# A two-layer gated network behind retention attention: own buffers in the opening, sums on another engine, other steps for weight preparation

## The chip, the cores and the metric

The kernel runs on one core of a Trainium2 chip. The metric is the time of one execution on the device, in microseconds. The engines are TensorE (PE, with its weight loads shown apart as PEld), VectorE (DVE), ScalarE (ACT), GpSimd (POOL) and SyncE (SP), which issues most transfers.

## The reference, cut to what matters

Everything is float32, weights come as float64. First comes attention with a decay, no softmax (4 batches, 8 heads, 576 positions, 64 features), whose output, laid side by side, is x with 2304 rows of 512:

```
scores = (q @ k.T) / sqrt(64)
x = (scores * Dmat) @ v           # Dmat[i, j] = gamma[h] ** (i - j) for i >= j, else 0
```

The first layer has 1536 hidden features, the second 2048:

```
xn  = x / sqrt(mean(x * x) + 1e-6) * rms_g
g   = xn @ w_gate
x   = (g * sigmoid(g) * (xn @ w_val)) @ w_out
h   = x @ w_in
g   = where(h >= 1, h, where(h <= -1, 0, (h + 1) ** 2 / 4))
out = g @ w_out2
```

## The kernel before

Attention runs in chunks of 128 positions (a tail of 64 ends each batch), 20 chunks in all, with a running `state` for each head. A chunk has two loads of 512 KB: load 2i holds q and k by feature, load 2i+1 holds k and v by position. `scores` of a chunk multiplies k with q on PE, scales q and k by powers of the decay on POOL (`qs`, `ks`) and multiplies the scores by the decay matrix on DVE (`ret`). `values` does the products with v and the state, copies x to `xraw` and adds up its squares (`sums`).

The first layer runs over five blocks of 512, 512, 384, 512 and 384 tokens, and for each block over 12 slices of 128 hidden features, one `step_a` each. Every float32 product is three products of a high and a low part (`split`: a cast on ACT, a subtraction on DVE; `three`: the matmuls). A step does two products with the normed x (`front`), the gate, and the last step's products into four accumulators (`back_a`). In the first block the weights are converted from float64 (`convert`) and stored; later blocks load them again. `prepare_norm` works out the next block's norm in step 9 (`NORM`). The attention chunks that the next block needs are done in the steps of the block before it; those of the first block, and three more (`AHEAD`), in the opening, ahead of all steps.

The second layer's first product uses Strassen's algorithm in Winograd's form: seven products of half-size blocks, with sums of weights (`prepare_in`, four sums of 128x256) and sums of x (`sums_x`, four sums of 128x768 for each group of 768 tokens). `prepare_in` and `prepare_out` convert and split the second layer's weights while the first layer runs, and store them to `wfd` and `wod`. There are 16 calls, by turns one and the other. They share `wpair` (converted weights), `wsum` (sums) and `wprep` (split weights).

The program text is not the order of issue. `Plan` takes every operation down with its dependencies and an assumed cost, works out when each is due, counted back from its users, and then writes out each engine's order. It simulates the engines and takes, on the engine that is free first, the ready operation that is due first; on PE the one that comes first in the text. A cost for one engine doesn't depend on what another does at the time.

Buffers in the opening: `place` gives each of the 40 attention loads its buffer. The first 14 take five buffers in turn: the three of `att_p`, then `wpair` and `wsum`. The odd chunks of the opening have their `ret`, `qs` and `ks` in the four tiles of the ring `t0`, `t1` (`opening`), and `rms_tiles` takes two scratch tiles from the same ring:

```python
early = [*buffers, wpair, wsum]
place = [early[i % len(early)] if i < 2 * ahead else buffers[i % ATT] for i in range(2 * len(chunks))]
opening = [t_p.tile([P, 512], F32, tag=g, name=g)[:, :] for g in ("t0", "t0", "t1", "t1")]
ret_b = [[...], opening[:2]]
```

Of the kernel before, what the change touches and what calls it, by code (L numbers as in the profile page):

```python
# [2 lines left out]

# [7 lines left out]
F32 = mybir.dt.float32  # L11
# [8 lines left out]
NT, DM, FA, FB = B * S, H * D, 1536, 2048  # L20
P = 128
KD = DM // P
# [16 lines left out]
NORM = NA - 3  # L39
ATT = 3  # L40
STAGE = 3


class Ring:
# [166 lines left out]
def moe_chain_kernel(ctx: ExitStack, tc: tile.TileContext, att, tail, wa, wb, dmat, gq, gk, out):  # L211
    nc = Plan(tc.nc)
    pool = lambda name, bufs, **k: Ring(ctx.enter_context(tc.tile_pool(name=name, bufs=1, **k)), bufs)
# [4 lines left out]
    ret_p = pool("ret", 1)  # L218
    stage_p = pool("stage", STAGE)
    w_p = pool("w", 2)  # L220
    wt_p = pool("wt", 2)
    one_p = pool("one", 1)
    h_p = pool("h", 3)
    xraw_p = pool("xraw", 2)
    t_p = pool("t", 2)
    r_p = pool("r", 1)
    sum_p = pool("sum", 2)
    sq_p = pool("sq", 1)
    o_p = pool("o", 2)
    ps_p = pool("ps", 1, space=PSUM)  # L230
    fr_p = pool("fr", 2, space=PSUM)
    dram_p = pool("dram", 1, space=DRAM)
# [4 lines left out]
    eps = const.tile([P, 1], F32, name="eps")  # L237
    ones = const.tile([P, P], F32, name="ones")
    state = const.tile([P, NPAIR, P], F32, name="state")
    xall = one_p.tile([P, 14 * 2 * TB], F32R, name="xall")  # L240
    wprep = one_p.tile([P, 8 * DM], F32R, name="wprep")
    wpair_w = one_p.tile([P, 2 * DM], U32, name="wpair")
    wsum_w = one_p.tile([P, 2 * DM], U32, name="wsum")
    wpair, wsum = (a[:, :].bitcast(F32) for a in (wpair_w, wsum_w))
    wa32 = dram_p.tile([NA, P, 3 * DM], F32, name="wa32")
    wfd = dram_p.tile([NPB, P, 14 * 2 * P], F32, name="wfd")
# [5 lines left out]
    def need(t):  # L252
        end = STARTS[t] + BLOCKS[t]
        return sum(b * S + c * CH < end for b in range(B) for c in range(NCH))
# [4 lines left out]
    stage_t, loaded, taken = {}, [0], [0]  # L259
    stages = [stage_p.tile([P, DM, 2], U32, tag="stage", name="st") for _ in range(STAGE)]  # L260
    more = [*stages, *(a.rearrange("p (n w) -> p n w", w=2) for a in (wpair_w, wsum_w))]
    stage_of = [more[i % len(more)] if 9 <= i < 3 * NA - 2 else stages[i % STAGE] for i in range(len(slots))]

# [27 lines left out]
    def split(src, hi, lo):  # L291
        nc.scalar.copy(out=hi, in_=src)
        nc.vector.tensor_sub(out=lo, in0=src, in1=hi.bitcast(F32))
# [24 lines left out]
    def a_weights(s, j):  # L318
        hi, lo = wt_t[s][:, :3 * DM], wt_t[s][:, 3 * DM:6 * DM]
        return hi[:, j * DM:(j + 1) * DM], lo[:, j * DM:(j + 1) * DM]  # L320

    def prepare_in(p):

        convert(wpair, 2)
        n = 2 * P
        a11, a12, a21, a22 = (wpair[:, i * n:(i + 1) * n] for i in range(4))
        s2, s1, s3, s4 = (wsum[:, i * n:(i + 1) * n] for i in range(4))
        nc.gpsimd.tensor_add(out=s1, in0=a21, in1=a22)
        nc.gpsimd.tensor_sub(out=s2, in0=s1, in1=a11)
        nc.gpsimd.tensor_sub(out=s3, in0=a11, in1=a21)  # L330
        nc.gpsimd.tensor_sub(out=s4, in0=a12, in1=s2)
        ready = wprep[:, :14 * n]
        hl = ready.rearrange("p (j w n) -> p j w n", w=2, n=n)
        for src, j0, j1 in ((wpair[:, :2 * n], 0, 2), (wsum, 2, 6), (a22, 6, 7)):
            src = src.rearrange("p (j n) -> p j n", n=n) if j1 - j0 > 1 else src.unsqueeze(1)
            split(src, hl[:, j0:j1, 0], hl[:, j0:j1, 1])
        nc.sync.dma_start(out=wfd[p], in_=ready.bitcast(F32))
# [18 lines left out]
    chunks = [(b, c) for b in range(B) for c in range(NCH)]  # L356
    first, ahead = need(0), need(0) + AHEAD
    buffers = [att_p.tile([P, 8 * CH], F32, tag="att") for _ in range(ATT)]
    early = [*buffers, wpair, wsum]
    place = [early[i % len(early)] if i < 2 * ahead else buffers[i % ATT] for i in range(2 * len(chunks))]  # L360
    opening = [t_p.tile([P, 512], F32, tag=g, name=g)[:, :] for g in ("t0", "t0", "t1", "t1")]
    ret_b = [[ret_p.tile([P, 4 * CH], F32, tag=f"ret{h}", name="ret")[:, :] for h in range(2)], opening[:2]]
    qs_b = [qk_p.tile([P, 4 * CH], F32, tag="qs", name="qs")[:, :], opening[2]]
# [28 lines left out]
    xraw, sums = {}, {}  # L392

    def x_slice(t):
        if t not in xraw:
            xraw[t] = xraw_p.tile([P, KD, 512], F32, tag="xraw", name="xraw")
            sums[t] = sum_p.tile([P, 512], F32, tag="sum", name="sums")
        return xraw[t], sums[t]

# [90 lines left out]


    def rms_tiles(T):
        tiles = t_p.tile([P, 512], F32, tag="t0"), t_p.tile([P, 512], F32, tag="t1"), r_p.tile([P, 512], F32, tag="y")
        return [a[:, :T] for a in tiles]

    def rms_rstd(t, ps):

# [50 lines left out]
    def back_a(s, i):  # L548
        _, t, f = steps[s]
        T = BLOCKS[t]  # L550
        oh, ol = a_weights(s, 2)
        hh, hl = h_t[s]
        if f == 0 and i == 0:
            acc_t[t] = [ps_p.tile([P, 512], F32, tag=f"acc{i}") for i in range(KD)]
        ps = acc_t[t][i]
        q = slice(i * P, (i + 1) * P)
        three(ps[:, :T], oh[:, q], ol[:, q], hh[:, :T], hl[:, :T], f == 0, f == NA - 1)
        if f == NA - 1:
            o = o_p.tile([P, 512], F32, tag="o", name="o")
            nc.scalar.copy(out=o[:, :T], in_=ps[:, :T])  # L560
            nc.scalar.dma_start(out=x2d[:, i, STARTS[t]:STARTS[t] + T], in_=o[:, :T])

# [13 lines left out]
    def step_a(s):  # L576
        _, t, f = steps[s]
        T = BLOCKS[t]
        goal = goals[t] if f < NORM else 0
        weights_split(s + 1, 0)  # L580
        if t and f % 2 == 0 and f < 8:
            prepare()
        g = front(s, 0)
        att_step(goal, "values")
        u = t_p.tile([P, 512], F32, tag="t0", name="u")
        w = t_p.tile([P, 512], F32, tag="t1", name="w")
        nc.scalar.activation(out=u[:, :T], in_=g[:, :T], func=ACTF.Sigmoid)
        nc.vector.tensor_mul(out=u[:, :T], in0=g[:, :T], in1=u[:, :T])
        v = front(s, 1)
        att_step(goal, "scores")  # L590
        nc.vector.tensor_mul(out=w[:, :T], in0=v[:, :T], in1=u[:, :T])
        if f == NA - 1 and t + 1 < len(BLOCKS):
            split_x(t + 1, 0, KD)
        h = h_p.tile([P, 4 * TB], F32R, tag="h", name="h")
        h_t[s] = h[:, :512], h[:, 512:1024]
        split(w[:, :T], h[:, :T], h[:, 512:512 + T])
        if s:
            back_a(s - 1, 0)
            back_a(s - 1, 1)
            prepare_norm(s)  # L600
            back_a(s - 1, 2)
            back_a(s - 1, 3)
        weights_split(s + 1, 1)
        weights_f32(s + 2)
# [15 lines left out]
    def load_x2(b):  # L620
        x2_t[b] = []
        for j in range(2):
            x = xraw_p.tile([P, KD, 512], F32, tag="xraw", name="x2")
            at = (2 * b + j) * TB
            nc.sync.dma_start(out=x[:, :, :TB], in_=x2d[:, :, at:at + TB])
            x2_t[b].append(x)
# [3 lines left out]
    def sums_x(b):  # L630
        x1, x2 = x2_t[b]
        b11, b21, b12, b22 = (x[:, k:k + 2, :TB] for x in (x1, x2) for k in (0, 2))
        three_d = lambda a: a.rearrange("p (k n) -> p k n", k=2)
        t1, t2 = three_d(wpair[:, :2 * TB]), three_d(wsum[:, :2 * TB])
        nc.gpsimd.tensor_sub(out=t1, in0=b12, in1=b11)
        nc.gpsimd.tensor_sub(out=t2, in0=b22, in1=t1)
        nc.gpsimd.tensor_sub(out=b12, in0=b22, in1=b12)
        t4 = three_d(gq_sb[:, :2 * TB])
        nc.gpsimd.tensor_sub(out=t4, in0=b21, in1=t2)
        xb_t[b] = [b11, b21, t2, t1, b12, b22, t4]  # L640

    xs = xall.rearrange("p (j w k n) -> p j w k n", w=2, k=2, n=TB)
# [24 lines left out]
    def back_b(q, i):  # L667
        b, p = divmod(q, NPB)
        if p == 0 and i == 0:
            acc_t["B", b] = [ps_p.tile([P, 512], F32, tag=g) for g in ("acc0", "acc1", "acc2", "acc3", "at0", "at1")]  # L670
        ps = acc_t["B", b][i]
        j, r = i * P // TB, slice(i * P % TB, i * P % TB + P)
        for f in range(2):
            hh, hl = h_t["B", q, f, j]
            w = wo_t[q, f]
            three(ps, hh[:, r], hl[:, r], w[:, :DM], w[:, DM:], p == 0 and f == 0, p == NPB - 1 and f == 1)
        if (i + 1) * P % TB == 0:
            for f in range(2):
                h_room.append(h_t.pop(("B", q, f, j)))
        if p == NPB - 1:  # L680
            o = o_p.tile([P, 512], F32, tag="o", name="o")
            nc.scalar.copy(out=o, in_=ps)
            r0 = (b * MT + i) * P
            nc.scalar.dma_start(out=out[r0:r0 + P, :], in_=o)
# [10 lines left out]
    def step_b(q):  # L695
# [47 lines left out]
        if p == 0 and b + 1 < NSB:  # L743
            load_x2(b + 1)
            sums_x(b + 1)
# [11 lines left out]
    while load_att():  # L757
        pass
    for i in range(STAGE):
        load_slot()  # L760
# [110 lines left out]
```

## Time and profile before

| what | before |
|---|---|
| median of 3 runs | 954.89 us (954.47 to 955.55) |
| the profiled execution's own time | 955.68 us |
| its span | 953.5 us |
| mean granted clock of TensorE | 0.981 |
| PE busy | 919.0 us (96%) |
| DVE busy | 575.8 us (60%) |
| ACT busy | 481.5 us (50%) |
| POOL busy | 123.9 us (13%) |

All times of the trace come from one profiled execution; times within it are counted from the first instruction. The span is from the first to the last instruction. Busy shares are means over stages with different limits, so what an engine's idle time is worth is read from the waits of each stage. In the rows below nearly every instruction has line L134, the helper that issues all operations; they are told apart by their tiles, written as out<-in.

### The profile page before, as it was taken

To read this page: it belongs to the slowest core of one execution; us is meant where nothing else is said; L and a number is where in the kernel's file an instruction comes from. 1 tells how busy PE (TensorE), PEld (TensorE's weight loads), DVE (VectorE), ACT (ScalarE), POOL (GpSimd) and SP (SyncE) were. 2 spreads that over 40 slices of the span, in tenths; PEclk is the share of its full clock that TensorE was granted. 3 is DMA by queue.
4 is the path that set the end of the run, shared out by engine and by line. 5 is a ranking of instruction groups with operands and counts; after the bars stand their busy time and mean duration, and the time that the engine had idled before them with its cause. 6 is when DMAs were issued, how large, how long until landed. Compare 5 with 4: busy or idle time off the path is not lost.

```text
span 953.5 us, 13338 instructions
## 1 busy us (share of the span) xinstructions
PE 919.0 (96%) x5098; PEld 809.4 (85%) x5098; DVE 575.8 (60%) x875; ACT 481.5 (50%) x852; POOL 123.9 (13%) x124
## 2 busy tenths in 40 slices
PE   7689999999999899999998999999999999999997
PEld 7567888888889798888898998899989898989896
DVE  4787889787887789644658554433653345534342
ACT  3444566645666565533544445344655455644443
POOL 4531001430214410200003001200030000000000
PEclk9779999999999899999999999999999999999999
DMA  9787874998868975522235359455675554756431
GB/s 352 273 296 249 273 271 161 380 350 291 307 223 351 359 279 200 182 78 100 100 132 177 133 194 346 166 180 185 224 272 193 172 206 159 243 188 210 154 133 66
DMA packets 50782, 209.94 MB, mean 220 GB/s; under 512 B 5536, under 2 KB 9760, under 8 KB 46624
## 3 DMA queue, kind: packets, MB, share of 16 engines
q1 hardware_dynamic: 44528, 198.72, 58.5%
q10 hardware_dynamic: 6192, 10.38, 2.9%
q8 instruction: 40, 0.66, 0.3%
q14 instruction: 22, 0.18, 0.1%
HBM read 167.14 MB, written 41.94 MB: 219 GB/s over the span
## 4 chain that ended last, share of the span: by engine, by line
PE 87%; DVE 5%; DMA 4%; ACT 2%; issue 2%; POOL 1%; ACTq 0%; DVEq 0%; SPq 0%; POOLq 0%
PE fr L134 48%; PE acc L134 28%; PE at L134 12%; DMA att<-in_att_dram 2%; DVE wt L134 1%; DMA x2d<-o 1%; DVE xall L134 1%; ACT att L134 1%; DVE t L134 0%; DVE w L134 0%; DMA out_dram<-o 0%; DMA gk_sb<-in_gk_dram 0%; DVE h L134 0%; ACT o L134 0%; DVE wpair L134 0%
## 5 line engine op out<-in xcount | busy, mean ns | idle before, releaser
L134 PE MATMUL fr<-xall,wt 128*128 128x384 f32 (+1 forms) x2424 | 516.2, 359 | 10.6 <-DVE t L134 3.5
L134 PEld LDWEIGHTS fr<-xall,wt 128*128 128x128 f32 x2424 | 442.2, 190 | 60.9 <-DVE wt L134 4.2
L134 PE MATMUL acc<-h,wt 128*128 128x512 f32 (+1 forms) x708 | 159.6, 372 | 0.1
L134 PE MATMUL acc<-wprep,h 128*128 128x512 f32 x576 | 156.1, 394 | 2.2 <-DVE h L134 1.8
L134 PEld LDWEIGHTS acc<-h,wt 128*128 128x128 f32 x708 | 128.3, 188 | 19.1 <-issue 0.7
L134 DVE TENSOR_TENSOR wt<-w,wt 128x512 fp32r<-128x512 f32 (+1 forms) x118 | 120.4, 1039 | 22.6 <-ACT wt L134 22.5
L134 ACT CAST wt<-w 128x512 fp32r<-128x512 f32 (+1 forms) x118 | 96.7, 834 | 59.5 <-PE acc L134 32.6
L134 PEld LDWEIGHTS acc<-wprep,h 128*128 128x128 f32 x576 | 106.6, 188 | 18.1 <-DVE h L134 2.1
L134 DVE TENSOR_TENSOR t<-fr,t 128x512 f32<-128x512 f32 (+1 forms) x120 | 76.2, 635 | 74.9 <-PE fr L134 40.0
L134 ACT ACTIVATE att<-att 128x384 f32<-128x384 f32 x156 | 79.1, 523 | 30.8 <-DVE att L134 20.9
L134 ACT CAST h<-t 128x512 fp32r<-128x512 f32 (+1 forms) x60 | 34.6, 576 | 77.5 <-DVE t L134 77.5
L134 DVE TENSOR_TENSOR h<-att,h 128x384 fp32r<-128x384 f32 x96 | 56.3, 591 | 25.3 <-ACT h L134 24.7
L134 PE MATMUL at<-wprep,h 128*128 128x512 f32 x288 | 70.3, 392 | 0.0
L134 DVE TENSOR_TENSOR att<-fr,att 128x384 f32<-128x384 f32 x48 | 26.6, 555 | 71.6 <-ACT att L134 70.3
L134 ACT ACTIVATE t<-fr 128x512 f32<-128x512 f32 (+1 forms) x60 | 33.3, 555 | 64.3 <-PE fr L134 64.0
L134 PEld LDWEIGHTS at<-wprep,h 128*128 128x128 f32 x288 | 53.7, 188 | 10.3
L134 ACT COPY att<-fr 128x384 f32<-128x384 f32 x48 | 23.0, 479 | 75.2 <-PE fr L134 71.9
L134 ACT CAST h<-att 128x384 fp32r<-128x384 f32 x96 | 48.7, 511 | 23.7 <-DVE att L134 22.5
L134 DVE SCALAR_TENSOR_TENSOR att<-att,att 128x384 f32<-128x384 f32 x48 | 28.0, 583 | 42.6 <-ACT att L134 42.6
L134 DVE TENSOR_TENSOR h<-t,h 128x512 fp32r<-128x512 f32 (+1 forms) x60 | 40.6, 677 | 14.6 <-ACT h L134 14.4
L134 POOL TENSOR_TENSOR wpair<-xraw,xraw 128x768 f32<-128x768 f32 x3 | 5.7, 1887 | 271.5 <-DMA xraw<-x2d 167.7
L134 POOL TENSOR_TENSOR wsum<-wpair 128x256 f32<-128x256 f32 x16 | 16.7, 1045 | 134.0 <-ACT y L134 62.9
(130 smaller groups left out, 734.6 us busy)
## 6 DMA issues: line engine op xcount, KB each, us to landing
w<-wa SPq DMA_DIRECT2D x48, 768.0 KB, 4.6
wprep<-wod SPq DMA_DIRECT2D x48, 512.0 KB, 4.3
wt<-wfd SPq DMA_DIRECT2D x24, 1024.0 KB, 5.2
wt<-wfd SPq DMA_DIRECT2D x24, 768.0 KB, 4.4
stage<-in_wb_dram SPq DMA_DIRECT2D x32, 512.0 KB, 5.9
att<-in_att_dram SPq DMA_DIRECT2D x29, 512.0 KB, 7.5
wfd<-wprep SPq DMA_DIRECT2D x8, 1792.0 KB, 6.8
stage<-in_wa_dram SPq DMA_DIRECT2D x26, 512.0 KB, 4.9
```

The source lines that it names most:

```text
L134: call = lambda: getattr(real, method)(*args, **kwargs)
```

## The change

Five edits:

- The first eight attention loads (chunks 0 to 3) get eight places of their own: the five of before, the two halves of the second `xraw` tile, and `o_sb`. Loads 8 to 13 go on in turn through the first five.
- `o_sb`, one tile of two halves, takes the place of the two `o` tiles: `next(o_next)` hands out the halves by turns for results on their way out. `rms_tiles` takes its two scratch tiles from the halves of `o_sb` as well, not from `t0` and `t1`. The two `xraw` tiles are fixed by index instead of by the ring.
- The four sums of `prepare_in` are done on DVE, not on POOL.
- The four sums of `sums_x` are done on DVE, not on POOL.
- `PREPARE` lists, block by block, the steps in whose text a `prepare` call stands. Before, each block but the first had steps 0, 2, 4 and 6; now the five blocks have 0, 4, 2, 4 and 6 calls.

```diff
+PREPARE = [(), (1, 3, 5, 7), (5, 7), (1, 3, 5, 7), (0, 1, 2, 3, 5, 6)]
...
-    o_p = pool("o", 2)
+    o_sb = one_p.tile([P, 2 * DM], F32, name="o")
+    o_next = itertools.cycle((o_sb[:, :DM], o_sb[:, DM:]))
...
-        nc.gpsimd.tensor_add(out=s1, in0=a21, in1=a22)
-        nc.gpsimd.tensor_sub(out=s2, in0=s1, in1=a11)
-        nc.gpsimd.tensor_sub(out=s3, in0=a11, in1=a21)
-        nc.gpsimd.tensor_sub(out=s4, in0=a12, in1=s2)
+        nc.vector.tensor_add(out=s1, in0=a21, in1=a22)
+        nc.vector.tensor_sub(out=s2, in0=s1, in1=a11)
+        nc.vector.tensor_sub(out=s3, in0=a11, in1=a21)
+        nc.vector.tensor_sub(out=s4, in0=a12, in1=s2)
...
-    early = [*buffers, wpair, wsum]
-    place = [early[i % len(early)] if i < 2 * ahead else buffers[i % ATT] for i in range(2 * len(chunks))]
+    xraws = [xraw_p.tile([P, KD, 512], F32, tag="xraw", name="xraw") for _ in range(2)]
+    flat = xraws[1].rearrange("p k n -> p (k n)")
+    early = [*buffers, wpair, wsum, flat[:, :1024], flat[:, 1024:], o_sb[:, :]]
+    place = [early[i] for i in range(8)] + [early[i % 5] for i in range(8, 2 * ahead)]
+    place += [buffers[i % ATT] for i in range(2 * ahead, 2 * len(chunks))]
...
-            xraw[t] = xraw_p.tile([P, KD, 512], F32, tag="xraw", name="xraw")
+            xraw[t] = xraws[t % 2]
...
-        tiles = t_p.tile([P, 512], F32, tag="t0"), t_p.tile([P, 512], F32, tag="t1"), r_p.tile([P, 512], F32, tag="y")
-        return [a[:, :T] for a in tiles]
+        return o_sb[:, :T], o_sb[:, DM:DM + T], r_p.tile([P, 512], F32, tag="y")[:, :T]
...
-            o = o_p.tile([P, 512], F32, tag="o", name="o")
+            o = next(o_next)
...
-        if t and f % 2 == 0 and f < 8:
+        if f in PREPARE[t]:
             prepare()
...
-            x = xraw_p.tile([P, KD, 512], F32, tag="xraw", name="x2")
+            x = xraws[j]
...
-        nc.gpsimd.tensor_sub(out=t1, in0=b12, in1=b11)
-        nc.gpsimd.tensor_sub(out=t2, in0=b22, in1=t1)
-        nc.gpsimd.tensor_sub(out=b12, in0=b22, in1=b12)
+        nc.vector.tensor_sub(out=t1, in0=b12, in1=b11)
+        nc.vector.tensor_sub(out=t2, in0=b22, in1=t1)
+        nc.vector.tensor_sub(out=b12, in0=b22, in1=b12)
...
-        nc.gpsimd.tensor_sub(out=t4, in0=b21, in1=t2)
+        nc.vector.tensor_sub(out=t4, in0=b21, in1=t2)
```

## Rows read from the trace of the kernel before

**Rows 1.** The page, busy time, share of the span and instructions of an engine:
```profile
PE 919.0 (96%) x5098; PEld 809.4 (85%) x5098; DVE 575.8 (60%) x875; ACT 481.5 (50%) x852; POOL 123.9 (13%) x124
```
**Rows 2.** Waits of PE, 0 to 70 us: total, times, longest
```profile
PE at L134 <- DVE t L134: 4.1, 3, 3.3
PE at L134 <- DMA att<-in_att_dram: 2.2, 2, 1.6
```
**Rows 3.** Timeline of the opening: start, duration, instruction [idle before <-releaser]
```profile
11.60 1.56 SPq L134 DMA_DIRECT2D att<-in_att_dram  x3
...
19.88 1.79 PE L134 MATMUL acc<-ret,att 128*64 128x128 f32 x16 [0.97 <-DMA att<-in_att_dram]
...
38.68 1.74 DVE L134 SCALAR_TENSOR_TENSOR t<-t,t 128x512 f32<-128x512 f32 x1
40.34 1.27 DVE L134 TENSOR_TENSOR t<-acc,d_sb 128x512 f32<-128x512 f32 x2
...
41.12 1.12 PE L134 MATMUL acc<-att,t 128*64 128x64 f32 x16 [5.12 <-issue]
```
**Rows 4.** Waits of PE, 281 to 388 us, the third block
```profile
PE fr L134 <- ACT wt L134: 3.3, 1, 3.3
PE fr L134 <- DVE t L134: 1.8, 1, 1.8
PE fr L134 <- DVE wt L134: 1.6, 2, 1.5
```
**Rows 5.** Waits of PE, 485 us to the end
```profile
PE acc L134 <- DVE h L134: 1.8, 1, 1.8
PE fr L134 <- DVE t L134: 1.7, 2, 1.5
PE fr L134 <- DVE wt L134: 1.2, 1, 1.2
```
**Rows 6.** Windows: length, busy PE, PEld, DVE, ACT, POOL; granted clock, DMA share, GB/s
```profile
10.00:40.00 30.00, 20.62 (x242) 17.63 (x242) 21.03 (x31) 13.24 (x23) 18.59 (x20) 0.83 0.97 372
40.00:70.00 30.00, 23.92 (x195) 20.23 (x196) 26.02 (x40) 14.63 (x25) 9.28 (x11) 0.79 0.70 242
140.00:281.00 141.00, 141.00 (x780) 116.15 (x780) 119.98 (x170) 84.64 (x130) 32.93 (x35) 1.00 0.77 283
281.00:388.00 107.00, 100.18 (x684) 93.03 (x680) 85.65 (x126) 62.12 (x102) 30.91 (x31) 0.97 0.80 301
```
**Rows 7.** The chain that ended last, in order of time: start, duration, what
```profile
69.07 5.22 PE fr L134 x18
...
325.34 10.72 PE fr L134 x46
340.63 8.26 PE fr L134 x46
...
485.11 4.18 PE fr L134 x24
...
521.61 5.66 PE fr L134 x22
```
**Rows 8.** The same windows, instructions on tile wsum alone (columns as Rows 6)
```profile
140.00:281.00 141.00, 0.00 (x0) 0.00 (x0) 6.09 (x5) 5.25 (x5) 19.58 (x20) 1.00 0.77 283
281.00:388.00 107.00, 0.00 (x0) 0.00 (x0) 4.49 (x3) 3.14 (x3) 12.46 (x12) 0.97 0.80 301
```
**Rows 9.** Timeline, one DVE subtraction of 128x256
```profile
323.20 0.41 DVE L134 TENSOR_TENSOR wprep<-wpair,wprep 128x256 fp32r<-128x256 f32 x1
```
**Rows 10.** Timeline of POOL and DVE at the first big sums
```profile
510.49 1.85 POOL L134 TENSOR_TENSOR wpair<-xraw,xraw 128x768 f32<-128x768 f32 x1 [103.75 <-DVE h L134]
510.64 2.51 DVE L134 TENSOR_TENSOR xall<-xraw,xall 128x768 fp32r<-128x768 f32 x1 [0.18 <-ACT xall L134]
...
521.95 0.95 DVE L134 TENSOR_TENSOR xall<-wsum,xall 128x768 fp32r<-128x768 f32 x1
```
**Rows 11.** Tile wfd, its stores: duration min/median/max ns, first and last start us
```profile
L134 SPq DMA_DIRECT2D wfd<-wprep x8: 319/320/327, 163.6 to 360.0; - x8
```

More of the change, by code (lines that the diff above doesn't have):

```diff
@@ L1 @@
-import heapq
+import itertools
 from contextlib import ExitStack
@@ L680, in back_b @@
         if p == NPB - 1:
-            o = o_p.tile([P, 512], F32, tag="o", name="o")
+            o = next(o_next)
             nc.scalar.copy(out=o, in_=ps)
```

## The prediction

> **What bounds the kernel now.** I read the page's first part first: TensorE (PE) is busy for 919.0 us, 96% of the span [rows 1]. So the matmuls are the bound almost everywhere, and an edit that adds no matmul and removes none can win only where PE stands idle or runs at its lower clock. Next come the waits of PE, stretch by stretch; the reader is to see that the idle time sits in three places. Before 70 us 4.1 us are for DVE and 2.2 for `att` transfers [rows 2], and one wait of 5.12 us has no releaser that the profile shows ("issue") [rows 3]. In the third block of the first layer (281 to 388 us) PE waits 3.3 + 1.8 + 1.6 = 6.7 us, for ACT and DVE [rows 4]. From 485 us to the end there are three more, 1.8 + 1.7 + 1.2 = 4.7 us [rows 5]. Last I read the busy times by stretch [rows 6]: DVE is the fullest engine beside PE, 120.0 of 141 us in the second block and 85.7 of 107 us in the third, and PE is never idle in the second. The granted clock is 0.83 and 0.79 of full speed (2.4 GHz) in the two opening stretches, a mean over its two levels, and 1.00 in the second block.
>
> The profiled execution took 955.68 us, 2.1 us around its span, and lies 0.8 us above the median of the runs shown (954.89). The sum is made against 955.7 and 0.8 us are taken off at the end. A run of this kernel tells a change from none at about 0.2%, or 1.9 us.
>
> **Part 1: the opening.** Attention loads 0 to 4 have five places; loads 5, 6 and 7 (the v half of chunk 2, both halves of chunk 3) must wait until loads 0, 1 and 2 are used up. They are issued only at 11.60 us, behind three weight loads [rows 3], and PE waits 0.97 us at 19.88 for the first of them [rows 3]. With own places they depend on nothing, and the planner, which issues by due time, puts them ahead of the three weight loads, whose first matmul comes after all chunks of the opening. Three loads of 512 KB at the 372 GB/s of this stretch [rows 6] are 4.2 us: so much earlier they land, and so much later the three weight loads. The later weights are covered: the first long run of matmuls on them starts at 69.07 us [rows 7]. Of the 2.2 us the longest, 1.6 us [rows 2], is at chunk 0 and stays; 0.6 us is for load 6. With the 0.97 that makes 1.6 us.
>
> The second edit in the opening is that `rms_tiles` takes its two scratch tiles from `o_sb`, not from the ring `t0`, `t1`. Until now those scratch tiles are also the `ret` buffers of the odd opening chunks. The rows show what that costs: the scratch op runs at 38.68 for 1.74 us, the multiply of chunk 5 (t<-acc,d_sb) follows only at 40.34, and PE, which needs both halves of it, starts again at 41.12 after 5.12 us idle [rows 3]. With its own scratch that multiply can run as soon as its scores are there. But DVE is near full then, 26.0 us busy of 30 from 40 to 70 [rows 6], so the wait is partly replaced by its queue. Bounds: 0 (DVE sets the pace of the whole opening, and everything won waits for DVE again) and all 5.1. I take 2.5, half. Beside the longest (3.3) the 4.1 us for DVE hold 0.8 [rows 2]; 0.6 of it, as I read it, is chunk 3's state product behind its late scores; it goes with the late load. The opening gives 1.6 + 2.5 + 0.6 = 4.7 us. Bounds for all of it: 0, and 9.0, the idle time of DVE from 10 to 40 us (30 - 21.03) [rows 6].
>
> **Part 2: the sums go from POOL to DVE.** There are 32 sums of 128x256, 20 in the second block and 12 in the third, 32.0 us on POOL together [rows 8], and 12 of 128x768 (four for each of three groups of tokens). DVE shows no such op by itself; the nearest rows are its subtractions of the same shapes with two SBUF inputs, 0.41 us for 128x256 [rows 9] and 0.95 us for 128x768 [rows 10]. So DVE gets 32 x 0.41 = 13.1 and 12 x 0.95 = 11.4 us, 24.5 us in all. What it gets back: while POOL runs a sum, a DVE op with two SBUF inputs is held. POOL starts at 510.49 and is done 1.85 us later, at 512.34; the DVE subtraction that starts at 510.64 takes 2.51 us and ends at 513.15, 0.81 us after POOL, while the same shape takes 0.95 us at 521.95 [rows 10]. One sum here costs DVE 1.6 us where it would cost 0.95 us on DVE itself. For DVE as a whole I take the move as neutral (bounds: nothing given back, +24.5 us, and the 1.6-for-0.95 of this row everywhere). What changes for PE is where the delays fall: the planner knows the cost of a sum on DVE, but not that a POOL op holds DVE, and now urgent DVE ops are late by up to 1.6 us at a time.
>
> By stretch. At 510 us the four sums of the second layer's first x: PE waits 1.7 + 1.2 = 2.9 us [rows 5], and the 22 matmuls after it take 5.66 us where 24 take 4.18 [rows 7], part of them at the lower level of the clock, to which it fell after the idle time: 5.66 - 22/24 x 4.18 = 1.8 us. Of 4.7 us I take 4.0, since four DVE ops of 0.95 us now stand in that queue (bounds 0 and 4.7). The same four sums for the second group of tokens stand beside the 1.8 us wait for `h` [rows 5]; I take 1.3 (bounds 0 and 1.8).
>
> In the third block the waits are 6.7 us, and 46 matmuls after them take 10.72 us where the next 46 take 8.26 [rows 7]: 2.4 us at the lower clock, 9.1 us in all. The sums of three prepares fall there. But the longest wait, 3.3 us, is for an ACT cast: ACT stood in front of an early rms matmul, and that is the order written by the planner and not POOL. A new plan may have such a spot again. Bounds: 9.1 gained, and 3 lost (one more such wait); I take half, 4.5.
>
> **Part 3: the chosen steps.** I cost it at nothing. Program order only sets dependencies; the order of issue is by due time. The preparations depend on each other (`wpair`, `wsum`, `wprep`, the stages), not on the step in which they are written. The trace says so: a quarter of them are written into the last block, which starts at 485.1 us [rows 7], yet the last store of `wfd` is issued at 360.0 [rows 11]. If the steps did matter, two preparations fewer would fall into the third block; its 9.1 us is the bound on that side and 0 the other. The x tiles of fixed index and the one `o` tile keep two buffers each; no queue is passed.
>
> **Sum.** 4.7 + 4.5 + 4.0 + 1.3 = 14.5 us. 955.7 - 14.5 - 0.8 = 940.4 us; its own range is 936 to 947.
>
> **Rivals.**
> (a) The opening gives nothing since DVE paces it, and the new plan puts a stall into the third block again: only 4.0 + 1.3 = 5.3 us stay, 949.6 us. For it speaks DVE's 26 of 30 us in [rows 6]; against it the 9 us that DVE is idle before.
> (b) DVE becomes the bound. In the second block PE has no idle time at all [rows 6], so there is nothing to win, only to lose: 20 of the 32 small sums are there and 12 in the third block. If each stands ahead of an op that PE needs, PE loses 13.1 us; the gains of part 1 (4.7) and the 5.3 us of the big sums remain: 955.7 + 13.1 - 10.0 - 0.8 = 958.0 us. It decides once DVE has no gap left to take the sums: it has 21 us in each of the two blocks [rows 6], against 20 x 0.41 = 8.2 and 12 x 0.41 = 4.9 us of sums. The Trainium skill (Perfetto Trace Analysis, Optimizing Scalar/DVE Operations) says that with DVE saturated, moving work to ScalarE or even GpSimd may make sense, which is this change backwards; it adds that the two share a read port, so that it might not help. The trace agrees with the second half (the held subtraction above), and by the first half alone the time would be 958.0.
> (c) All the waits of the third block go, and the opening gains what DVE allows: 9.0 + 9.1 + 4.7 + 1.8 = 24.6 us, 930.3 us.
> (d) The planner's new order gives back what it gains: no change, 953 to 957.
>
> **Chances.** Forecast (936 to 947) 0.47, (a) (947 to 953) 0.20, (c) (under 936) 0.13, (d) 0.07, (b) 0.13. Faster by over 0.2%: 0.80; within: 0.07; slower: 0.13. The range is 930 to 955: below it a part of (c), above it (b) and the upper end of (d), together under 0.2.
>
> **What would show it.** Right: in the opening, the v load of chunk 2 landing ahead of the weights and no wait of PE for it; the multiply of chunk 5 not behind the scratch op; steady matmuls at least 4 us earlier. No DVE subtraction of 128x768 above 1 us near the big sums, and PE without a wait there. `wfd` stores at nearly the same times. Wrong: PE waits for DVE in the second block; a new wait for ACT in the third; or an opening that starts its long run of matmuls at 69 us as before.

## The result and the profile after

The changed kernel takes 923.56 us (922.26 to 923.88), a ratio of 0.9657 to the kernel before, interval [0.9628, 0.9687]: about 32 us less, where 14.5 were forecast. The sign was right, the size was not, and the time lies under the range.

The busy times by stretch (columns as [rows 6]), in the same two opening stretches, then the third block and the last block of the changed kernel:

```profile
10.00:40.00 30.00, 23.76 (x320) 19.21 (x320) 21.60 (x35) 15.24 (x29) 20.93 (x24) 1.00 0.92 339
40.00:70.00 30.00, 28.58 (x225) 23.03 (x226) 26.48 (x42) 14.82 (x26) 10.52 (x12) 1.00 0.68 234
260.54:385.98 125.44, 125.21 (x880) 115.30 (x879) 105.81 (x165) 74.19 (x123) 23.43 (x25) 1.00 0.74 272
460.11:537.11 77.00, 77.00 (x442) 76.49 (x440) 49.66 (x70) 36.47 (x59) 0.00 (x0) 1.00 0.49 166
```

The clock is at full speed in both opening stretches, against 0.83 and 0.79 in [rows 6], and PE has almost no idle time in the third block and none in the last. The waits of PE over the whole span of the changed kernel:

```profile
PE at L135 <- DMA att<-in_att_dram: 1.4, 1, 1.4
PE fr L135 <- DVE xall L135: 1.3, 1, 1.3
PE at L135 <- DVE t L135: 1.3, 1, 1.3
PE fr L135 <- POOL sum L135: 1.2, 1, 1.2
...
PE acc L135 <- ACT h L135: 0.5, 1, 0.5
...
PE fr L135 <- DVE wt L135: 0.2, 1, 0.2
```

All above 0.6 us are in the opening; of [rows 4] only 0.2 us for `wt` is left and of [rows 5] nothing. The timeline of the opening, changed kernel:

```profile
8.95 0.80 SPq L135 DMA_DIRECT2D xraw<-in_att_dram  x2
...
10.18 0.33 SPq L135 DMA_DIRECT2D o<-in_att_dram  x1
...
11.79 1.28 SPq L135 DMA_DIRECT2D stage<-in_wa_dram  x3
...
18.91 1.09 PE L135 MATMUL acc<-ret,xraw 128*64 128x128 f32 x16
...
25.80 1.13 PE L135 MATMUL fr<-sum,ones 128*128 128x512 f32 x2 [1.17 <-POOL sum L135]
...
28.36 1.28 DVE L135 TENSOR_TENSOR t<-acc,d_sb 128x512 f32<-128x512 f32 x2
...
29.56 0.68 DVE L135 SCALAR_TENSOR_TENSOR o<-o 128x512 f32<-128x512 f32 x1
...
35.74 0.96 PE L135 MATMUL fr<-xall,wt 128*128 128x512 f32 x3 [0.27 <-ACT xall L135]
```

Loads 5, 6 and 7 stand in SP's queue ahead of the three weight loads, PE has their data without a wait (18.91, against 0.97 us in [rows 3]), and the multiply of chunk 5 now stands ahead of the scratch op. The norm matmul of the first block (fr<-sum,ones) starts at 25.80; in the kernel before at 33.79.

For all comparisons below I count matmuls: a step of the first layer has 24 on `xall` (two products, four slices, three each), so step s begins with number 24s+1 of them. From the profiled runs, in us (blocks begin with steps 0, 12, 24, 36 and 48; the second layer is from step 60 on):

| kernel | ratio to before, interval | step 0 at | step 12 at | step 24 at | steps 24-39 | steps 48-60 | second layer |
|---|---|---|---|---|---|---|---|
| before | 1 | 45.7 | 163.7 | 276.8 | 134.0 | 82.5 | 386.1 |
| changed | 0.9657 [0.9628, 0.9687] | 35.7 | 150.1 | 260.5 | 125.4 | 77.0 | 383.4 |
| open_only | 0.9781 [0.9751, 0.9810] | 37.2 | 151.6 | 262.1 | 131.9 | 82.6 | 387.6 |
| place_only | 0.9792 [0.9766, 0.9819] | 37.8 | 151.6 | 264.1 | 128.0 | 82.6 | 389.4 |
| rms_only | 0.9938 [0.9915, 0.9962] | 45.3 | 160.4 | 273.3 | 132.3 | 83.7 | 387.5 |
| sums_only | 0.9866 [0.9844, 0.9889] | 45.9 | 163.9 | 278.6 | 131.1 | 77.0 | 383.2 |
| place_old | 0.9826 [0.9811, 0.9840] | 45.8 | 164.9 | 277.7 | 127.7 | 77.0 | 383.8 |
| pin_pool | 0.9689 [0.9673, 0.9705] | 35.7 | 150.0 | 260.4 | 128.1 | 77.0 | 383.5 |
| sx_pool | 0.9727 [0.9710, 0.9745] | 37.9 | 153.3 | 263.8 | 125.7 | 82.6 | 385.8 |
| fill_before | 0.9989 [0.9972, 1.0005] | 42.6 | 161.0 | 274.2 | 134.0 | 83.5 | 387.9 |
| late_issue | 0.9783 [0.9768, 0.9798] | 49.4 | 158.9 | 271.4 | 128.3 | 77.0 | 383.8 |
| weights_last | 0.9805 [0.9788, 0.9822] | 41.5 | 150.6 | 263.8 | 126.6 | 83.9 | 387.4 |
| wl_sums | 0.9683 [0.9662, 0.9705] | 42.9 | 151.9 | 264.4 | 125.5 | 77.5 | 383.3 |

Steps 39 to 48 take 74.1 us in each. The 33.0 us of span (953.5 to 920.5) are 16.3 up to step 24, 8.6 in steps 24 to 39, 5.5 in the last block and 2.6 in the second layer (before rounding). Up to step 24 PE is busy for 259.75 us of 276.82 before and 251.58 of 260.54 after, with the same 1578 matmuls: 8.1 us less idle time, and 8.2 us less for the same work, which I put down to the clock (granted 0.96 of full speed in that stretch before, 1.00 after).

The columns of times come from one execution each, and in the opening one execution does not repeat another. Kernels with the same order of instructions up to 144 us or more came as far apart as this at step 12: 150.0, 150.1, 151.6 and 153.3 us with the new order (pin_pool, changed, open_only, sx_pool); 162.6 to 165.0 with the old one (before, and three kernels further below that leave the opening alone); 160.4 and 164.9 in rms_only and place_old. The granted clock goes with it: 0.87 from 40 to 70 us in rms_only, 0.73 in place_old. So a difference of 10 us up to step 24 is one of the kernels, and a difference under some 4 us need not be. Where the order is the same, the stretches from step 24 to step 60 repeat within 1 us and the second layer within some 2 us.

### The profile page after: what moved, and what is told of

Read it like the earlier page. It is cut to its first block, busy times and chain, and to the rows that moved or that the text cites. A ratio compares the mean times of both kernels' runs of the same rounds, so it can differ in the third digit from the quotient of the medians.

```text
span 920.5 us, 13305 instructions
## 1 busy us (share of the span) xinstructions
PE 905.6 (98%) x5098; PEld 798.5 (87%) x5098; DVE 574.0 (62%) x919; ACT 480.5 (52%) x852; POOL 70.4 (8%) x80
## 4 chain that ended last, share of the span: by engine, by line
PE 92%; DMA 3%; DVE 2%; ACT 1%; issue 1%; POOL 0%; ACTq 0%
PE fr L135 50%; PE acc L135 30%; PE at L135 11%; DMA x2d<-o 1%; DMA att<-in_att_dram 1%; DVE xall L135 0%; DMA out_dram<-o 0%; DMA gk_sb<-in_gk_dram 0%; DVE xraw L135 0%; ACT o L135 0%; DVE t L135 0%; ACT att L135 0%; DVE w L135 0%; DVE wt L135 0%; DVE o L135 0%
## 5 line engine op out<-in xcount | busy, mean ns | idle before, releaser
L135 PEld LDWEIGHTS fr<-xall,wt 128*128 128x128 f32 x2424 | 437.3, 188 | 51.9 <-DVE xall L135 2.4
L135 PEld LDWEIGHTS acc<-h,wt 128*128 128x128 f32 x708 | 128.3, 188 | 18.2
L135 DVE TENSOR_TENSOR wt<-w,wt 128x1024 fp32r<-128x1024 f32 (+1 forms) x118 | 115.1, 987 | 25.1 <-ACT wt L135 24.5
L135 ACT CAST wt<-w 128x1024 fp32r<-128x1024 f32 (+1 forms) x118 | 96.9, 835 | 52.5 <-PE acc L135 30.0
L135 DVE TENSOR_TENSOR h<-att,h 128x384 fp32r<-128x384 f32 x96 | 52.8, 554 | 23.8 <-ACT h L135 23.2
L135 DVE SCALAR_TENSOR_TENSOR att<-att,fr 128x384 f32<-128x384 f32 x24 | 13.3, 554 | 35.3 <-ACT att L135 35.3
L135 DVE TENSOR_TENSOR xall<-xraw,xall 128x512 fp32r<-128x512 f32 (+2 forms) x32 | 26.0, 828 | 2.6 <-ACT xall L135 2.4
```

The costliest lines, as they stand in the source:

```text
L135: call = lambda: getattr(real, method)(*args, **kwargs)
```

## The experiments

### Which part does it

Three kernels with the changed places and the new scratch, both or one at a time, with sums on POOL and the old steps:

```diff
 open_only   # early, place, o_sb as changed; sums on gpsimd; f % 2 == 0 and f < 8
 place_only  # the same, and
-        return o_sb[:, :T], o_sb[:, DM:DM + T], y
+        return t0[:, :T], t1[:, :T], y      # the ring's tiles
 rms_only    # open_only, and
-    place = [early[i] for i in range(8)] + [early[i % 5] for i in range(8, 2 * ahead)]
+    place = [early[i % 5] for i in range(2 * ahead)]
```

> Only the opening is changed: own places for loads 0 to 7, and the scratch tiles of the norm in o_sb; all sums stay on POOL, the steps of the preparations are the old ones. Theory 1 (the parts act each in their own stretch): step 12 comes about 16 us earlier, as in the changed kernel, the granted clock stays at full speed in the opening, the later stalls stay (third block, last block): 936 to 940 us. Theory 2 (the new order of the whole plan made the gain, no part by itself): a time that has nothing to do with 16 us, under 5 us gained or over 25.

> Only the eight own places; the norm's scratch tiles stay in the ring t0, t1 and the sums on POOL. If the late loads were what made the opening slow: 8 us or more gained, step 0 at about 38 us. If the shared scratch was: under 4 us, and a long wait of PE behind the multiply of chunk 5 stays.

> Only the norm's scratch tiles move to o_sb; loads 5 to 7 wait for used places as before, sums on POOL. If the shared scratch made the opening slow: 8 us or more gained. If the late loads did: under 4 us, and step 0 no earlier than 43 us.

Measured: 21 us for both parts, 20 for the places alone, 6 for the scratch alone. The places make the opening. rms_only is the miss for my reading of [rows 3]: with a scratch of its own the multiply of chunk 5 still stands behind the scratch op on DVE, and PE waits just as long, 5.07 us. Its timeline:

```profile
37.75 1.44 POOL L135 TENSOR_TENSOR qs<-att,gq_sb 128x512 f32<-128x512 f32 x1
37.99 1.75 DVE L135 SCALAR_TENSOR_TENSOR o<-o 128x512 f32<-128x512 f32 x1
39.66 1.28 DVE L135 TENSOR_TENSOR t<-acc,d_sb 128x512 f32<-128x512 f32 x2
...
40.40 1.93 PE L135 MATMUL acc<-t,att 128*64 128x128 f32 x12 [5.07 <-DVE t L135]
```

What held the multiply was its place in DVE's queue, not the shared tile. In place_only, where the tile is still shared, the wait is gone. The rows show something more that the working had passed over: the scratch op takes 1.75 us here with a POOL op on two SBUF tensors beside it, and ends 0.55 us after that op; in the changed kernel, with POOL idle, the same op takes 0.68 (29.56 above). A part of this wait is POOL holding DVE, as with the sums below.

The sums alone, on the kernel before:

```diff
-        nc.gpsimd.tensor_add(out=s1, in0=a21, in1=a22)   # and the seven others
+        nc.vector.tensor_add(out=s1, in0=a21, in1=a22)
```

> The kernel before with the sums of weights and of x on DVE, nothing else. Theory 1: the opening is as slow as before (step 12 within 1 us of 163.7), the later waits go: 16 to 17 us gained, 937 to 940 us. Theory 2: stalls come back at other places in the third block, 945 us or more. The forecast's own term for this part was 9.8 us.

Measured 13 us (0.9866; 945.8 us beside a kernel before of 959.0), by its gain between the two expectations: the opening is unchanged (step 12 at 163.9), the last block takes 77.0 us and the second layer 383.2, as in the changed kernel, but the third block keeps 5.7 of its 8.6 us.

Three that undo one part of the changed kernel:

```diff
 pin_pool    # prepare_in: nc.vector back to nc.gpsimd
 sx_pool     # sums_x: nc.vector back to nc.gpsimd
 place_old   # place = [early[i % 5] for i in range(2 * ahead)], five places
```

> The changed kernel with the four sums of the weights back on POOL; the sums of x stay on DVE. If those sums make the waits of the third block: 5 to 7 us slower than the changed kernel (a ratio of about 0.972 to the kernel before), all of it between steps 24 and 39; last block and second layer as in the changed kernel. If they do nothing: within 1 us of the changed kernel (0.966).

> The changed kernel with the four sums of x back on POOL; the sums of the weights stay on DVE. If a POOL sum holds DVE: the last block (steps 48 to 60) takes 82.6 instead of 77.0 us and the second layer 386 to 388 instead of 383.4, so 8 to 10 us slower than the changed kernel (a ratio of about 0.975). If only the new order made that gain: under 4 us.

> The changed kernel with five places in turn for the first 14 loads, as before; the norm's scratch tiles stay in o_sb. If the late loads made the opening slow: step 12 at 160 us as with the scratch tiles alone, so 10 us slower than the changed kernel (a ratio of about 0.976). If the sums on DVE shorten the opening as well: 5 us or less.

pin_pool is 2.7 us longer in the third block and the same elsewhere: half of what was expected; over whole runs its interval overlaps that of the changed kernel. sx_pool has the last block back at 82.6 and the second layer at 385.8 us (8.0 together, as expected). Its step 24 comes 3.3 us late as well, but up to 380 us every engine has the same instructions in the same order as in the changed kernel: that is the difference between two executions, not an effect of the edit. place_old has the old opening, 164.9. Over all the kernels of the table the last block takes 82.5 to 83.9 us where the sums of x are on POOL and 77.0 to 77.5 where they are on DVE, and the second layer 385.8 to 389.4 and 383.2 to 383.8, whatever else differs. In sx_pool's timeline at these sums, first DVE, then POOL:

```profile
489.27 0.96 DVE L135 TENSOR_TENSOR xall<-xraw,xall 128x768 fp32r<-128x768 f32 x1 [0.18 <-ACT xall L135]
490.19 2.30 DVE L135 TENSOR_TENSOR wt<-w,wt 128x512 fp32r<-128x512 f32 x1
492.40 2.61 DVE L135 TENSOR_TENSOR xall<-xraw,xall 128x768 fp32r<-128x768 f32 x1
```
```profile
489.76 2.17 POOL L135 TENSOR_TENSOR wpair<-xraw,xraw 128x768 f32<-128x768 f32 x1 [104.87 <-DMA xraw<-x2d]
492.01 2.19 POOL L135 TENSOR_TENSOR wsum<-xraw,wpair 128x768 f32<-128x768 f32 x1
```

The split of `wt` starts at 490.19 and ends 0.56 us after the POOL op (491.93); alone it takes 0.69. In the changed kernel the same stretch reads, on DVE:

```profile
485.80 0.96 DVE L135 TENSOR_TENSOR xall<-xraw,xall 128x768 fp32r<-128x768 f32 x1 [0.18 <-ACT xall L135]
486.71 0.69 DVE L135 TENSOR_TENSOR wt<-w,wt 128x512 fp32r<-128x512 f32 x1
487.32 0.95 DVE L135 TENSOR_TENSOR wpair<-xraw,xraw 128x768 f32<-128x768 f32 x1
```

A sum costs DVE 0.95 us, the price taken from [rows 10], and the urgent op beside it is not stretched. The Trainium skill (SBUF — State Buffer, SBUF: two separate sides) has DVE and GpSimd share one port pair, which one op holds whole while the other is blocked; these rows agree.

### Why the places matter: the order of the loads

Two kernels separate a place from the time at which a load lands. late_issue keeps the own places and puts the loads back behind the three weight loads; weights_last has the old places and puts the three weight loads behind loads 5 to 9. The planner gets new dependencies for it, and in weights_last the three loads are also written later in the text:

```diff
 late_issue   # changed kernel, in load_att, for loads 5, 6, 7
+        if 5 <= i < 8:
+            nc.ops[-1][2].add(use_at[i - 5])     # last matmul in the text up to the use of load i - 5
 weights_last # kernel before, in load_slot, for the first three weight loads
+            if i < STAGE:
+                nc.ops[-1][2].update(freed)      # load 7 comes first
...
-    for i in range(STAGE):                       # now with the first `convert`
-        load_slot()
```

> The changed kernel, own places kept, but loads 5, 6 and 7 stand behind the three first weight loads in the queue of SP, because the planner is told that each has to follow the use of load 0, 1 or 2, as before. If the time at which these three loads land makes the opening: norm matmul (fr<-sum,ones) at 30 us or later instead of 25.8, step 12 at 155 us or later, 5 to 10 us slower than the changed kernel. If it is the other freedom that own places give (loads 10 to 12 find their buffers free early): step 12 within 2 us of 150.1.

> The kernel before with its five places, but the three first weight loads stand behind loads 5 to 7 and the two of chunk 4 in the queue of SP. Nothing else is changed. If the landing time of loads 5 to 7 makes the opening: norm matmul at 27 to 30 us instead of 33.8, step 12 some 6 to 10 us earlier than 163.7, 945 to 950 us beside a kernel before of 955. If own places are needed (a buffer that comes free late): under 2 us.

weights_last is the clearest run of the study: without any own place step 12 comes at 150.6 (150.1 in the changed kernel) and the kernel takes 0.9805 of the time, 19 us less. Its timeline, SP and PE:

```profile
8.78 4.26 SPq L134 DMA_DIRECT2D att<-in_att_dram  x3
13.78 0.56 SPq L134 DMA_DIRECT2D wsum<-in_tail_dram  x1
15.88 0.34 SPq L134 DMA_DIRECT2D wpair<-in_tail_dram  x1
16.27 1.38 SPq L134 DMA_DIRECT2D stage<-in_wa_dram  x3
20.79 1.30 SPq L134 DMA_DIRECT2D att<-in_att_dram  x2
...
27.91 1.13 PE L134 MATMUL fr<-sum,ones 128*128 128x512 f32 x2 [1.06 <-POOL sum L134]
...
34.98 1.98 PE L134 MATMUL acc<-t,att 128*64 128x128 f32 x16 [3.42 <-DVE t L134]
```

The three weight loads stand behind five attention loads, the attention loads after them move up too (from 20.79 on, against 22.96 before), and the norm matmul is 5.9 us earlier. Of PE's 5.1 us wait for chunk 5's multiply 3.42 us are left here.

late_issue gives back 8.8 of the 13.6 us at step 12, and its norm matmul comes at 39.36 us. It does not restore the old order, though:

```profile
8.88 1.53 SPq L135 DMA_DIRECT2D stage<-in_wa_dram  x3
11.74 0.33 SPq L135 DMA_DIRECT2D xraw<-in_att_dram  x1
12.18 0.36 SPq L135 DMA_DIRECT2D att<-in_att_dram  x1
12.59 0.43 SPq L135 DMA_DIRECT2D o<-in_att_dram  x1
13.12 0.36 SPq L135 DMA_DIRECT2D att<-in_att_dram  x1
13.67 0.33 SPq L135 DMA_DIRECT2D xraw<-in_att_dram  x1
```

Two of loads 10 to 12 (`att`) overtake the last of loads 5 to 7 (`xraw` at 13.67). Its norm is later than in the kernel before (33.79), and yet its step 12 is 4.8 us earlier. That an early landing of loads 5 to 7 counts is shown. How the gain divides between them and loads 10 to 12, which come early in late_issue and in weights_last too, was not tested, and the 4.8 us stay open.

weights_last with the sums on DVE as well has no own place and no `o_sb`:

> The kernel before with the three first weight loads behind loads 5 to 9 (as in weights_last) and all sums on DVE: no own places, no o_sb, old steps. If the order of those loads and the sums are all of the change: 922 to 928 us, a ratio of about 0.966 to 0.97, as the changed kernel. If own places are needed beside the order: 932 us or more.

At 0.9683 the interval overlaps that of the changed kernel: the order of the attention loads against the weight loads, and the engine of the sums, are nearly all of the change. Own places are one way to get that order.

### The clock in the opening

> The kernel before in its old order, with 30 matmuls of ones by ones (0.4 us each, into a bank that nothing reads) put into the places of the opening where PE waited, each run of them a little shorter than the wait: 4 before the values of chunk 0, 2 + 2 in chunk 2, 1 before the scores of chunk 3, 1 in chunk 3, 2 in chunk 4, 11 in chunk 5, 7 in chunk 7. No wait is removed. If half of the opening's gain is the clock, which falls because PE stands idle: the clock stays high in the opening and step 24 comes 5 to 8 us earlier than at 276.8. If the clock is no part of it and only the waits count: step 24 within 1 us, or later.

```diff
+            for bank, lhsT, n in self.fill.get(i, ()):      # in issue, ahead of the marked matmul
+                for _ in range(n):
+                    self.raw.matmul(bank[:, :P], lhsT=lhsT, rhs=lhsT, start=True, stop=True)
```

Windows of fill_before (columns as [rows 6]):

```profile
0.00:58.00 58.00, 47.71 (x520) 41.21 (x520) 42.61 (x63) 24.44 (x42) 27.39 (x32) 1.00 0.86 326
58.00:70.00 12.00, 10.98 (x52) 9.45 (x51) 8.88 (x15) 5.32 (x8) 3.36 (x4) 0.57 0.84 275
```

The clock stays full up to 58 us (0.88 in that window of the kernel before) and falls after that as before. Step 24 is 2.7 us earlier, under the 5 to 8 expected, and the total is not measurably different. PE is busy for 262.84 us up to there, 8.6 of them with the fill: the same 1578 matmuls take 254.2 us, 5.5 less than before, but only half of that reaches step 24; the rest comes back as waits. And 2.7 us is no more than two executions of one order differ by. So filling the waits kept the clock and made the matmuls faster, but no gain in time from it is shown; the fall after 58 us was not removed, and its share could not be measured alone.

### The longest wait of the third block

I had put the 3.3 us wait for ACT down to a norm matmul that the planner moves ahead. Two edits on the kernel before, alone and together: the norm's matmul tied to the matmul ahead of it in the text, and the `wfd` store of 306.0 us cut short.

```diff
 norm_pinned      # in rms_rstd, for the blocks
+            nc.ops[-1][2].add(last)              # last: the matmul ahead of it
 no_store         # sixth wfd store: [:, :P] of 3584 columns; read back from the fifth
 pinned_no_store  # both
```

> The kernel before, with the norm's matmul in the blocks tied to its place in the text (the planner may not move it ahead of the matmul that stands before it). If the early norm matmul, with ACT waiting for it, makes the longest wait of the third block: the 3.3 us wait for ACT wt goes and steps 24 to 39 take 129 to 131 instead of 134.0 us. If the wait comes from the sums on POOL: 133 us or more.

> The kernel before in its own order of issue, with one store cut short: the sixth store of wfd (issued at 306.0 us, 1792 KB) writes 64 KB, and the second layer reads the fifth in its place. If the 3.3 us wait of the third block comes from weight loads (w<-wa) that land late in a full transfer queue: that wait shrinks to 1 us or less and steps 24 to 39 take 129 to 131 us instead of 134.0. If ACT's order or the sums on POOL make it: 133 us or more and the wait stays.

> Both edits at once: the norm's matmul tied to its place (norm_pinned) and the sixth wfd store cut short (no_store; it writes 64 KB of 1792, and the second layer reads the fifth in its place). If the 3.3 us wait has two causes, each enough by itself (ACT behind the norm, and the weight load landing at 321.5 us in a full transfer queue), it goes only now: 1 us or less, and steps 24 to 39 take 129 to 131 us. If neither is the cause: the wait of 3 us stays again and the steps take 133 us or more.

norm_pinned: 1.0026 [1.0001, 1.0050], steps 24 to 39 in 135.0 us, the wait 3.4 us. no_store: 0.9995 [0.9983, 1.0008], 134.3 us, the wait 3.3. Both theories miss. But in norm_pinned ACT waits for something else; from its timeline:

```profile
322.74 1.05 ACT L134 CAST wt<-w 128x1024 fp32r<-128x1024 f32 x1 [2.01 <-DMA w<-wa]
```

The weights of the next step have not landed. Together the edits do what neither does alone: 0.9964 [0.9946, 0.9981], steps 24 to 39 in 130.8 us, as expected, and the wait is 1.3 us, a little over the 1 us that I had allowed:

```profile
PE fr L134 <- DVE t L134: 2.4, 2, 1.8
PE fr L134 <- DVE wt L134: 1.6, 2, 1.5
PE fr L134 <- ACT wt L134: 1.3, 1, 1.3
```

So that wait has two causes, each enough for most of it: ACT stands in front of the early norm, and a weight load lands late in a full transfer queue.

### Attempts at a faster kernel

> The changed kernel with the two adds of squares of chunks 0 to 3 on DVE instead of POOL: an attempt at a faster one. POOL is the releaser of two waits of 1.2 and 0.9 us in the opening. If DVE can take eight more ops of 0.3 to 0.4 us there: 1 to 3 us faster than the changed kernel. If DVE sets the pace of the opening: 0 to 3 us slower.

> The changed kernel with the three first weight loads behind all loads of chunks 3, 4 and 5 (loads 7 to 12): an attempt at a faster one. If earlier attention loads still help: step 12 one to three us earlier than 150.1. If the weights are then late for the first steps: slower by 2 us or more.

> The changed kernel with the norm's matmul tied to its place in the text: an attempt at a faster one. The changed kernel has no wait in the third block that a norm could make: within 2 us of it (0.966), in either direction, if the order is as good; worse by 2 us or more if the planner's freedom there fills gaps.

```diff
 after_sq      # changed kernel, in values
+                add = (nc.vector if i < first else nc.gpsimd).tensor_add   # both adds of squares
 after_wl      # changed kernel, weights_last's edit, behind load 9; first conversion one chunk later in the text
 after_pinned  # changed kernel, norm_pinned's edit
```

after_sq 0.9730 [0.9703, 0.9758] and after_wl 0.9732 [0.9702, 0.9761] are slower than the changed kernel, both in the opening (step 12 at 155.2 and 156.2); after_pinned, 0.9673 [0.9646, 0.9700], is no faster. None beats it. For loads 5 to 7 a place ahead of the weights is worth some 13 us at step 12, for the next five less than nothing; whether the weights then come late or only another plan comes out is not shown.

## Why the prediction was wrong

- **Part 1, late loads: the step that failed.** The prediction counted as their cost the waits of PE that the profile puts down to `att` transfers, 1.6 us, and 0.6 for chunk 3. But the loads delayed the whole chain behind them (scores, state, squares, norm), and most of that delay shows as waits for DVE, the state or "issue". A better measure would have been the start of the norm matmul: 33.8 before, 25.8 after, and 27.9 with nothing but the order of loads changed (late_issue, with 39.4 and a step 12 between the two, shows that it is not a measure of everything). The working even had 4.2 us as the time by which the loads come earlier, and did not carry it down the chain.
- **Part 1, scratch: wrong cause.** The 5.1 us wait was put down to the shared tile and half of it counted. It stays at 5.1 with a scratch of its own, is 3.4 with the weight loads moved and gone with own places. Beside own places the scratch is worth nothing that can be measured (0.9781 and 0.9792). Without them it is worth 4 to 6 us over whole runs (rms_only; place_old against sums_only), by what path stays open.
- **Part 1, the bound of 9.0 us was none.** It was DVE's idle time before 40 us. Up to step 24 the gain is 16.3. Half of it, 8.2 us, is less PE time for the same matmuls, although 0.83 and 0.79 stood in [rows 6]: a stall was priced by its length alone in the opening, while in the two later blocks the slow matmuls behind it were counted. That the clock stays up because the waits are shorter is argued, not shown; and fill_before, which won 5.5 us of such time and at most half of it in time, shows that the two halves do not simply add.
- **Part 2, last block and second layer: right in mechanism, too small.** 4.0 and 1.3 forecast, 5.5 and 2.6 measured. The price of a sum on DVE was right (0.95 us), and its four ops in the queue cost PE nothing.
- **Part 2, third block: 4.5 forecast, 8.6 measured, inside its bound of 9.1.** The named spot was right, its cause was half right: the norm, and a late weight load. The sums of weights are worth 2.7 us there (pin_pool against the changed kernel). weights_last does without most of these waits with all sums on POOL (126.6 us). How much the opening's order and the sums each take off depends on the plan, and their parts don't add (2.1 + 2.9 alone, 8.6 together); that stays open.
- **Part 3: right.** With the old steps the changed kernel has the same instructions in the same order on every engine; it is the same program and was not run. The stores of `wfd` in the changed kernel, beside [rows 11]:

```profile
L135 SPq DMA_DIRECT2D wfd<-wprep x8: 319/326/327, 158.8 to 385.3; - x8
```

- **Rivals.** (b), DVE as the bound, did not come: DVE is busy for 105.8 of 125.4 us in the third block and PE for 125.2. The rule that would take work from a full DVE to GpSimd (the Trainium skill, Perfetto Trace Analysis, Optimizing Scalar/DVE Operations) would have cost here: sx_pool, which does that with the sums of x, is slower (0.9727), and pin_pool is 2.7 us slower in its trace. (c) was nearest, at 930.3.

## What to carry to other kernels

A load that lands late costs as much as the chain behind it is delayed, not as much as the wait that carries its name: follow it to a milestone, as the first norm here, and try the order of the queue before spending memory on buffers; three weight loads moved behind five attention loads gave 19 of 32 us. A small elementwise op on POOL beside a busy DVE is not free work if DVE's ops read two SBUF tensors: price it by the stretched op beside it. A stall that lets PE's clock fall makes the matmuls behind it slower too; how much of that reaches the end has to be measured. And a milestone from one execution is worth no more than the difference between two executions of the same order, up to 4.5 us here.

## What the runs showed of the hardware

The fill matmuls kept the clock full through 58 us of an opening in which it had fallen twice, and the same matmuls took 5.5 us less, yet step 24 moved by only 2.7 us: there, at least half of the time lost at the lower clock was hidden in waits for other engines. And a wait can have two releasers that hide each other: the profile named ACT in one kernel and the transfer behind it in the next.
